# Linear attention with a feed-forward block: loading q and k as they are and casting them on the engines, with a new order of work

## The chip, the core and the metric

The kernel runs on one core of one Trainium2 chip. The metric is the device time of one execution in microseconds; smaller is better. TensorE (PE) does the matmuls, VectorE (DVE), ScalarE (ACT) and GpSimd (POOL) the elementwise work, and SyncE (SP) mostly issues transfers. Each engine works through its own queue in order.

## The reference

Inputs are q, k and v of shape (8, 8, 576, 64), that is batch, head, token and channel, a matrix w_phi (64 x 128), a gain g (512) and the two weights w1 (512 x 2048) and w2 (2048 x 512). All are float32, and the output is (8, 576, 512) in float32.

```python
def phi(x):
    proj = einsum('bhsd,df->bhsf', x, w_phi)
    proj = proj - max(abs(proj), axis=-1, keepdims=True)
    return concatenate([exp(proj), exp(-proj)], axis=-1)
q_p, k_p = phi(q), phi(k)
kv  = einsum('bhsf,bhsd->bhfd', k_p, v)
z   = sum(k_p, axis=2)
num = einsum('bhsf,bhfd->bhsd', q_p, kv)
den = einsum('bhsf,bhf->bhs', q_p, z)[..., None] + 1e-06
x   = (num / den) with the heads side by side        # (8, 576, 512)
xn  = (x - mean(x)) / sqrt(var(x) + 1e-6) * g
out = x + maximum(xn @ w1, 0) @ w2
```

## The kernel before, in words

**Tiling.** The work is cut into 32 units, n = 0 to 31. A unit is one head position of two batches (in the first half of the kernel) or two heads, so that two sequences of 576 tokens fill the 128 partitions as 9 tiles of 128: 8 full tiles ("main") and one tile that is shared by the last 64 tokens of both ("tails", or "mixed"). Eight units make a pair of batches. When a pair's attention is done, its tokens go through layer norm and the feed-forward block (`moe_block`), in blocks of two or three tiles of 128 tokens: `L1307` is the first layer's matmul (hT_ps from xT and w1), `L1337` the second layer's (ch_ps from hT and w2). So attention of one pair and the feed-forward work of the pair before lie side by side.

**Steps of one unit.** (1) Loads of k, q and v: `load_main` for the eight full tiles, `load_tails` for the tails of four units at a time, both through `issue` (L516) on SP. (2) q and k are turned so that the channel lies on the partitions. For n < 8 (`a_trans`, L684 and L692) PE transposes and DVE or ACT copies out of PSUM. For n of 8 and more (`a_trans_dma`) a transposing DMA on SP does it (L766), from a bf16 copy of q and k of 1152 columns: k main, q main, and the mixed tile of both (`cast_mixed`, run by DVE at L747, ACT at L751 or POOL at L753, 128 x 128). (3) k's features (`a_k`): projections pk (L828) and n_bank (L786, L787), their largest magnitude by DVE (`m`, L834 and L790), exponentials on ACT (`eb`, L844 and L799), and the scaled values `vv` on POOL (L856, L865, L869). (4) kv (L1025, L1030). (5) q's features (`a_q` or `a_qt`: L973, L978, L990, L997). (6) num, its copy and division on DVE (numc, L1087 and L1092; rden, L1096) and POOL (x and xs, L1102). Half of the shared tile has to move to other partitions: ACT issues that transfer (x<-xs, L1162). The statistics of layer norm follow on DVE (st, L1220).

**bf16 of q and k, before.** For n of 8 and more, `load_cast` (L598) has GpSimd issue a DMA for each of k and q that reads float32 and writes bf16. It writes into places of 1152 columns inside the three float32 buffers `qk0` to `qk2`, which the first eight units no longer need (`place`, `b16_of`, `freed`), nine in all. Five units ahead of the turned one they may be issued. v has four buffers of its own (`VB`), of two units each.

**Order of work.** Nobody writes the order of instructions down: `add` and `dma` put operations with their engines, an estimate of their duration, dependencies and a rank into the object `Order`, and `Order.run` is a list scheduler that plays the program forward. Whenever an engine is free it takes the waiting operation of lowest rank; where several engines may do an operation (a tuple such as ("DVE", "ACT", "POOL")), the first to come free takes it. The rank is the latest time by which the operation should be done (worked out backward from its users) and an offset from the table `OFF` (by stage and step), or a fixed number for the first loads. DMAs have rings of limited depth in this model, and GpSimd's counts twice as deep in both kernels:

```python
full = op.dma and out.get(op.dma[0], 0.0) + op.dma[1] > self.RING * (1 + (engine == "POOL"))
```

SP's loads for units 4 to 7 are held behind a small read of w1's second part, and those from unit 8 on behind one of w2's first part (`gate`, L528), so that they don't come ahead of the weights. w1 and w2 are loaded by POOL with a cast to bf16, 512 KB at a time (L651 for w2). While PE has nothing else to do early on, it gets matmuls without use[...] (L1537).

Of the kernel before, what the change touches and what calls it, by code (L numbers as in the profile page):

```python
# [17 lines left out]
def bcast(ap: bass.AP, dim: int, n: int) -> bass.AP:  # L18
# [11 lines left out]
        0: 92.8, 1: 85.3, 2: -3301.7, 3: -3074.5, 4: 39.4, 5: 575.5, 6: -409.6, 7: 15.1,  # L30
        8: -3043.8, 9: -3397.9, 10: -8.4, 12: -2030.6, 13: -226.3, 14: 37.5,
    },
    "gln": {
        0: 142.3,
    },
    "k": {
        1: 91, 2: 352.8, 3: 1027.1, 4: -300.7, 5: -347.8, 6: -303.3, 7: -15.4, 8: 86.1, 9: -803.6,
        10: 307.3, 11: 67, 12: 872.6, 14: 68.9,
    },
    "k.copy": {  # L40
        0: 27.5, 1: 624.4, 2: 1020, 3: -41.9, 4: -146.3, 5: -130.6, 6: -93.2, 7: -12.2,
    },
    "k.em": {
        0: 66.7, 1: -12.4, 2: -2704.1, 3: -5.5, 4: 2583.9, 5: 720, 6: 527.6, 7: 686.5, 8: 39.7,
        9: 1215.1, 10: 22.4, 11: -37.6, 12: -46.9, 13: 19.3, 14: -59.6,
    },
    "k.exp": {
        0: 188.2, 1: 599.5, 2: -1722.2, 3: 1885.9, 4: 237, 5: 319.5, 6: 867.4, 7: -1027.3, 8: 71.8,
        9: -954.6, 10: 387.6, 11: 330.1, 12: -2543.4, 13: 63.5, 14: -1109,
    },  # L50
    "k.max": {
        0: 1569, 1: -946.9, 2: 273.7, 3: -20.5, 4: 114.3, 5: 327.6, 6: 1009.3, 7: 1002.8, 8: -0.8,
        9: 1094.3, 10: 10.7, 11: 59, 12: -68.6, 13: -951.5, 14: -1127.6,
    },
    "k.trans": {
        0: -7.2, 1: -1022.5, 2: -632.1, 3: -783.7, 4: -590.8, 5: -463.7, 6: 32.6, 7: -241.5,
    },
    "kv": {
        0: 195.3, 1: 553, 2: -28, 3: -16.8, 4: 270.9, 5: -60.9, 6: 223.5, 7: -39.9, 8: 365.9,
        9: -223.3, 10: -4.4, 11: 20.5, 13: 781.1, 14: -117.9,  # L60
    },
    "kv.copy": {
        0: 237.8, 1: 62, 2: 2860.6, 3: 321.8, 4: 63.3, 5: 2519.7, 6: -15.2, 7: 158.4, 8: -131.4,
        9: -19.3, 10: -60.7, 11: -587.9, 12: -21.5, 13: -167.8, 14: 75.9,
    },
    "ln": {
        1: -186.3, 3: -357.5, 5: 320.2, 7: 225.2, 9: 872.1, 11: 348.5, 12: -181.6, 13: 9.5,
        14: 504.1,
    },
    "load": {  # L70
        0: 156.7,
    },
    "load.k": {
        13: 485.9, 14: 14.4,
    },
    "load.q": {
        12: -258.4, 13: -36.4, 14: -10.1,
    },
    "mixed": {
        0: -130.9, 1: 150.4, 2: 88.2, 3: 843.9, 4: -116.4, 5: -307.5, 6: -40.2, 7: 826.8, 8: -91.9,  # L80
        9: -92.9, 10: -88.2, 11: -759.1, 12: -1174.8, 13: 671.4, 14: 538.1,
    },
    "mixed.exp": {
        0: 927.2, 1: 863, 2: 1200.3, 3: -3220.2, 4: -589.9, 5: -59.5, 6: 740.3, 7: 376.2,
        8: -1565.6, 9: 1094.8, 10: 177.3, 11: -410.5, 12: -3506.5, 13: -1650.3, 14: -105.6,
    },
    "mixed.max": {
        0: -192.1, 1: -703.2, 2: -4.1, 3: -338.5, 4: 2.6, 5: -110.2, 6: -686.6, 7: -22.7, 8: -884,
        9: -2824.2, 10: -192.1, 11: -325.5, 12: -2773, 13: -359.5, 14: -96.5,
    },  # L90
    "num0": {
        0: 668.5, 1: 34.9, 2: -83.4, 3: 342.5, 4: 198.5, 5: -1847.5, 6: -169.5, 7: -294.1,
        8: -20.2, 9: -175.7, 10: 80.8, 11: -1536.1, 12: -48.4, 13: -960, 14: 329,
    },
    "num0.dve": {
        0: 467.7, 1: -325.6, 2: 1058.4, 3: -480.5, 4: -143.5, 5: -456.9, 6: 380.8, 7: 367.2,
        8: -351.2, 9: 1035.8, 10: -367.2, 11: 206.3, 12: -1071.3, 13: -466.6, 14: -343.4,
    },
    "num0.put": {
        0: 158.5, 1: 162.1, 2: 714.5, 3: 1000, 4: 2127.5, 5: 919.3, 6: 170.2, 7: 534.6, 8: 380,  # L100
        9: -292.9, 10: 618.1, 11: -171.9, 12: -129.4, 13: -653.3, 14: -2.8,
    },
    "num1": {
        0: 64.3, 1: -596, 2: -654, 3: -332.2, 4: -1102.9, 5: 475.6, 6: -590.7, 7: -265.9,
        8: -276.4, 9: -9.7, 10: -480.3, 11: -935.2, 12: -521.5, 13: 777.3, 14: 1011.8,
    },
    "num1.dve": {
        0: 84.4, 1: -186.2, 2: -460.6, 3: -1840.9, 4: -2161.8, 5: -395.2, 6: -105.8, 7: -549.4,
        8: -2.1, 10: 97.7, 11: -25.5, 12: -2301.1, 13: -1093.4, 14: -1.7,
    },  # L110
    "num1.put": {
        0: -179.5, 1: -61.8, 2: 860.1, 3: 859.5, 4: 319.2, 5: 1040.7, 6: 995.3, 7: -110.8, 8: 32.3,
        9: -352.4, 10: -61.7, 11: -84, 12: -1.1, 13: -1343.5, 14: 97.8,
    },
    "q.copy": {
        0: 330.4, 1: 30.2, 2: 127.5, 3: -31.8, 4: -79.4, 5: -134.6, 6: -426.1, 7: 529.3,
    },
    "q.em": {
        4: 45.3, 5: -61.4, 6: -188.6, 7: 270.2, 8: 315.4, 9: -17.4, 10: 711.1, 11: 298.7, 12: 22.3,
        13: -76.3, 14: 190.2,  # L120
    },
    "q.max": {
        4: -193.9, 5: -101.7, 6: -240.1, 7: -51.2, 8: -277.1, 9: 20.7, 10: 28.1, 11: -94.7,
        12: -13.8, 13: 92.4, 14: -11.3,
    },
    "q.trans": {
        0: 45.5, 1: -159.9, 2: -531.4, 3: -292.7, 4: -479.2, 5: 176.8, 6: -2243.6, 7: 121,
    },
    "q0": {
        0: 79.7, 1: -34.4, 2: -5.9, 3: -201.1,  # L130
    },
    "q0.em": {
        0: 76.9, 1: 41.6, 2: 606.2, 3: 231.2,
    },
    "q0.max": {
        0: 825, 1: 421.3, 2: 60, 3: 1085.5,
    },
    "q1": {
        0: 197.7, 1: -2405.6, 2: -288.3, 3: -2131.6,
    },  # L140
    "q1.em": {
        0: 238.1, 1: -58.7, 2: -5.1, 3: 4.8,
    },
    "q1.max": {
        0: 427.7, 1: 596.9, 2: 514.4, 3: -33,
    },
    "qt": {
        4: 43, 5: 53.1, 6: -128.5, 7: -1504.6, 8: -3097.5, 9: -1391.5, 10: 114.9, 11: -626.5,
        12: -2970.3, 13: -7.3, 14: -54.6,
    },  # L150
    "rstd": {
        0: 91.5, 8: -236.3, 13: -445.4, 14: 145.7,
    },
    "tails.exp": {
        4: -752.5, 5: -3.9, 6: -0.8, 7: 208.6, 8: 178.4, 9: 354.6, 10: 602.6, 11: -955.4,
        12: -21.2, 13: 639, 14: 303.5,
    },
    "tails0": {
        0: 131.9, 1: -217.5, 2: -9.9, 3: -31.5,
    },  # L160
    "tails0.exp": {
        0: 154.5, 1: -6.8, 2: 62.7, 3: -457.1,
    },
    "tails1": {
        0: 362.3, 1: 805.6, 2: -360.7, 3: 151.6,
    },
    "tails1.exp": {
        0: 149.3, 1: 342, 2: -76.5, 3: 132.1,
    },
    "trans": {  # L170
        8: -2185.6, 10: -214.5, 11: 486.6, 12: 2328, 13: 336.2, 14: 2841.3,
    },
    "vv": {
        0: 1911, 1: -32.9, 2: 1483.8, 3: -49.4, 4: -503, 5: -400, 6: 190.2, 7: 127.9, 8: -262.5,
        9: -99.4, 10: -2335.1, 11: -1439.8, 12: -298.5, 13: -874.4, 14: -529.5,
    },
    "w1": {
        12: -982.9,
    },
    "x.copy": {  # L180
        0: 42.2, 1: -374.1, 2: 474.8, 3: -258.7, 4: -65, 5: 735.5, 6: -171, 7: -70.5,
    },
    "x.trans": {
        0: 934.9, 1: 1052.1, 2: 752.8, 3: 133.9, 4: 1973, 5: 59, 6: 1165, 7: 495.3,
# [11 lines left out]
class Order:  # L196
# [31 lines left out]
    def backward(self):  # L228
        for op in reversed(self.ops):
            us = sum(op.us) / len(op.us) + op.lag  # L230
            if op.dma:
                us += op.dma[1] * op.dma[2] + self.START + self.LAND
            users = [o for o in op.users if not (o.dma and o.engines == ("POOL",))]
            late = min((o.late for o in users), default=1000.0) - us
            op.late = late if op.due is None else min(late, op.due)
# [129 lines left out]
def kernel(  # L365
# [38 lines left out]
    NBUF, VB = 3, 4  # L404
# [44 lines left out]
    for i in range(VB):  # L449
        v_bufs.append(consts.tile([P, HG, MX * D], FP32, name=f"v{i}"))  # L450
# [30 lines left out]
    qkT_bufs = [consts.tile([P, ST], BF16, name=f"qkT{i}") for i in range(QB)]  # L481
    wst = consts.tile([P, F], BF16, name="wst")
# [55 lines left out]
    def load_main(key, n, nu, rank, queue):  # L538
# [4 lines left out]
        slot = g % (VB if key == "v" else NBUF)  # L543
        buf = v_bufs[slot] if key == "v" else qk_bufs[slot][:, "qk".index(key)]
        dst = buf[:, u0 : u0 + nu, :]
        us = range(u0, u0 + nu)
        if pair < SPLIT:
# [7 lines left out]
                [(key + str(half), slot, u) for u in us for half in range(2)]  # L555
# [5 lines left out]
        for half in range(2):  # L561
            b, h, _ = heads(pair, i, half)
            src = bass.AP(
                tensor=t.tensor, offset=t.offset + (b * H + h) * S * D,
                ap=[[4 * D, P], [S * D, nu], [1, 4 * D]],
            )
            issue(
                queue, rank, dst[:, :, half * 4 * D : (half + 1) * 4 * D], src,
                [(key + str(half), slot, u) for u in us], 131072 * nu, gated=gate_of(n),
            )  # L570

    def place(n):
        i = (n - QK_DMA) % (3 * NBUF)
        return i, (i // 3 + 1) % NBUF

    def b16_of(n):
        i, j = place(n)
        flat = qk_bufs[j].rearrange("p a u f -> p (a u f)").bitcast(BF16)
        return flat[:, i % 3 * ST : i % 3 * ST + ST]

    def freed(n):
        if n >= QK_DMA + 3 * NBUF:
            return []
        return [("freed", place(n)[1], u, i) for u in range(HG) for i in range(2)]

    def load_cast(key, n):

        t, i = {"q": q, "k": k}[key], "qk".index(key)
        b, h, _ = heads(n // H, n % H, 0)
        src = bass.AP(  # L590
            tensor=t.tensor, offset=t.offset + (b * H + h) * S * D,
            ap=[[4 * D, P], [S * D if n // H < SPLIT else H * S * D, 2], [1, 4 * D]],
        )
        dst = b16_of(n)[:, i * 512 : (i + 1) * 512].rearrange("p (a f) -> p a f", a=2)
# [980 lines left out]
```

## Time and profile before

| | |
|---|---|
| time, median of 3 runs | 385.69 us (384.36 to 385.82) |
| the profiled execution | 385.82 us, of which the span 384.0 us |
| TensorE clock granted, mean | 0.996 |
| PE busy | 361.3 us, 94% |
| DVE, ACT, POOL busy | 287.3, 233.0, 193.8 us |
| first layer's matmuls L1307, second layer's L1337 | 151.9 and 149.9 us |
| POOL's 48 issues of casting loads (L598) | 24 of 727 ns for k, 24 of 749 ns for q |
| casting loads, from issue to landing, median | k 6.6, q 5.2 us |
| transposing DMAs of q and k (L766) | 24, median 4.6 us to landing |

The page gives busy time by engine, then the span in 40 slices of 9.6 us, a digit being tenths of busy time. A group's row has the line, the engine, the operation, what it writes and reads, the number of instructions, then busy time in us, the mean of one in ns, the idle time of the engine ahead of it and what ended that. A row of the waits has the engine and line that waited, what it waited for, the total in us, the number of times and the longest. Issuing a DMA isn't counted as busy in the first section.

### The profile page before, as it was taken

What the parts mean: (1) busy time and instruction counts of PE and PEld (TensorE: products, weight loads), DVE (VectorE), ACT (ScalarE), POOL (GpSimd) and SP (SyncE); (2) the same over time, 40 slices, a digit from 0 to 9 for tenths busy, and PEclk for the clock granted to TensorE, in tenths of its full rate; (3) what the DMA queues carried; (4) which work ended last, traced back from release to release, by engine and by line L of the source; (5) the groups of instructions that cost most, each with busy time, mean ns of one, the idle gap of its engine ahead of it and who ended that gap; (6) DMA issues with size and microseconds to landing.
All of it is one profiled execution on the core that took longest, in us unless ns stands there. A gap on an engine that the chain in (4) does not pass through costs nothing.

```text
span 384.0 us, 9310 instructions
## 1 busy us (share of the span) xinstructions
PE 361.3 (94%) x3559; PEld 231.0 (60%) x3559; DVE 287.3 (75%) x630; ACT 233.0 (61%) x549; POOL 193.8 (50%) x391
## 2 busy tenths in 40 slices
PE   8899988868989899999999999999999999999995
PEld 8789766524756566655756665665665555555543
DVE  6689977738979798888888896978877956454522
ACT  4879977546879798997867769675665522000000
POOL 2754899735587999895775563432462100000000
PEclk9999999998999999999999999999999999999999
DMA  6998399990699999998977508315100252110102
GB/s 187 270 214 301 58 178 227 175 208 6 142 188 164 199 146 194 185 146 190 152 158 120 137 29 140 76 22 76 46 30 29 43 123 68 29 55 29 54 28 84
DMA packets 93101, 47.08 MB, mean 123 GB/s; under 512 B 59520, under 2 KB 88576, under 8 KB 93056
## 3 DMA queue, kind: packets, MB, share of 16 engines
q1 hardware_dynamic: 74112, 35.60, 41.0%
q0 software_dynamic: 17280, 10.49, 20.5%
q10 hardware_dynamic: 1664, 0.39, 0.5%
q8 instruction: 28, 0.46, 0.5%
q14 instruction: 17, 0.14, 0.1%
HBM read 36.77 MB, written 9.44 MB: 120 GB/s over the span
## 4 chain that ended last, share of the span: by engine, by line
PE 70%; DMA 14%; POOL 5%; SPq 4%; DVE 3%; ACT 2%; issue 1%; DVEq 0%; ACTq 0%; POOLq 0%
PE ch_ps L1337 27%; PE hT_ps L1307 25%; DMA qkT<-qk 4%; PE n_bank L1030 3%; SPq L516 3%; DMA qx<-in_q_dram 3%; PE pk L828 3%; PE num L1073 2%; PE n_bank L1537 2%; POOL vv L856 2%; POOL x L1102 2%; DMA x<-xs 2%; PE pq L973 2%; DMA qk<-in_k_dram 2%; DMA w<-in_moe_w_ch_dram 2%
## 5 line engine op out<-in xcount | busy, mean ns | idle before, releaser
L1307 PE MATMUL hT_ps<-xT,w 128*128 128x384 bf16 (+1 forms) x832 | 151.9, 313 | 4.4 <-ACT hT L1317 2.1
L1337 PE MATMUL ch_ps<-w,hT 128*128 128x512 bf16 (+1 forms) x592 | 149.9, 375 | 0.6 <-DVE hT L1315 0.6
L1307 PEld LDWEIGHTS <-w 128*128 128x128 bf16 x832 | 76.9, 98 | 52.8 <-issue 7.6
L1315 DVE TENSOR_SCALAR hT<-hT_ps 128x384 bf16<-128x384 f32 (+1 forms) x137 | 72.0, 528 | 45.6 <-PE hT_ps L1307 44.1
L1102 POOL TENSOR_TENSOR x<-numc,rden 128x192 bf16<-128x192 f32 (+4 forms) x112 | 49.8, 461 | 73.5 <-DVE rden L1096 62.0
L856 POOL TENSOR_TENSOR vv<-v,em 128x512 bf16<-128x512 f32 x60 | 62.7, 1045 | 42.5 <-issue 18.6
L1337 PEld LDWEIGHTS <-hT 128*128 128x128 bf16 x592 | 54.8, 98 | 45.2 <-issue 3.2
L1317 ACT ACTIVATE hT<-hT_ps 128x384 bf16<-128x384 f32 (+1 forms) x71 | 32.5, 457 | 65.7 <-PE hT_ps L1307 65.2
L844 ACT ACTIVATE eb<-pk 128x1024 bf16<-128x1024 f32 x64 | 65.1, 1033 | 6.0 <-DVE m L834 3.8
L997 ACT ACTIVATE ea<-pt 128x1024 bf16<-128x1024 f32 x56 | 56.7, 1026 | 14.1 <-PE pt L978 13.6
L834 DVE TENSOR_REDUCE m<-pk 128x8 f32<-128x1024 f32 x32 | 38.9, 1217 | 4.5 <-PE pk L828 4.4
L990 DVE TENSOR_REDUCE m<-pq 128x8 f32<-128x1024 f32 x28 | 34.0, 1215 | 4.1 <-PE pq L973 4.1
L1344 DVE SCALAR_TENSOR_TENSOR o<-ch_ps,rstd,x 128x512 f32<-128x512 f32 (+1 forms) x37 | 26.8, 729 | 13.0 <-PE ch_ps L1337 9.7
L1220 DVE BATCH_NORM_STATS2 st<-x 128x6 f32<-128x256 bf16 (+1 forms) x52 | 25.4, 515 | 7.4 <-DMA x<-xs 5.5
L1073 PEld LDWEIGHTS <-ea 128*128 128x128 bf16 x512 | 25.1, 97 | 8.1 <-issue 0.7
L1030 PE MATMUL n_bank<-vv,eb 128*128 128x65 bf16 x512 | 26.8, 194 | 0.0
L1244 ACT ACTIVATE xc<-x,mv 128x512 bf16<-128x512 bf16 x32 | 21.8, 734 | 6.7 <-DVE o L1344 5.1
L1030 PEld LDWEIGHTS <-eb 128*128 128x128 bf16 x512 | 22.3, 98 | 5.5 <-issue 2.2
L869 POOL TENSOR_TENSOR vv<-vx,em 128x130 bf16<-128x130 f32 x63 | 25.2, 400 | 0.0
L1537 PE MATMUL n_bank<-wz 128*128 128x120 bf16 x306 | 23.7, 228 | 0.6 <-ACT KV L1039 0.5
L828 PE MATMUL pk<-wbk,qkT 128*128 128x256 bf16 x128 | 19.8, 279 | 4.2 <-DVE m L990 4.2
L1537 PEld LDWEIGHTS <-wz 128*128 128x128 bf16 x306 | 20.1, 105 | 0.7 <-issue 0.5
(91 smaller groups left out, 451.4 us busy)
## 6 DMA issues: line engine op xcount, KB each, us to landing
out_dram<-o SPq DMA_DIRECT2D x31, 256.0 KB, 2.5
v<-in_v_dram SPq DMA_DIRECT2D x24, 256.0 KB, 3.8
w<-in_moe_w_ch_dram POOLq DMA_DIRECT2D x8, 512.0 KB, 10.3
qk<-in_k_dram POOLq DMA_DIRECT2D x24, 128.0 KB, 6.6
qk<-in_q_dram POOLq DMA_DIRECT2D x24, 128.0 KB, 5.2
qk<-in_k_dram SPq DMA_DIRECT2D x8, 256.0 KB, 5.4
qk<-in_q_dram SPq DMA_DIRECT2D x8, 256.0 KB, 6.5
v<-in_v_dram SPq DMA_DIRECT2D x4, 512.0 KB, 9.3
```

The lines of the kernel that those rows point to most:

```text
L834: nc.vector.reduce_max(out=u["m"][:, 1, 0:MX], in_=u["pk"], axis=AX.X, apply_absolute_value=True)
L844: nc.scalar.activation(u["EB"][:, t, 0:MX, :], u["pk"], AF.Exp, scale=(1.0, -1.0)[t])
L856: eng.tensor_tensor(out=u["vv"][:, t, 0:MX, 0:D], in0=vb[:, hh, :].rearrange("p (c d) -> p c d", d=D), in1=bcast(e[:, 0:MX], 2, D), op=ALU ...
L990: nc.vector.reduce_max(out=out, in_=ps, axis=AX.X, apply_absolute_value=True)
L997: nc.scalar.activation(u["EA"][:, t, :], u["pt", None], AF.Exp, scale=(1.0, -1.0)[t])
L1030: nc.tensor.matmul(ps[:, t, c // 4, :], EB[:, t, c, :], vv[:, t, c, :], start=False, stop=(t == 0 and c == MX - 1), skip_group_check=True,)
L1073: nc.tensor.matmul(ps[t][:, i, :], ea(u, t, c), KV[:, t, c // 4, :], start=True, stop=True,)
L1102: nc.gpsimd.tensor_tensor(out=dst, in0=st["numc"][ps_, at, 0:D], in1=bcast(st["rden"][ps_, at], 2, D), op=ALU.mult,)
L1307: nc.tensor.matmul(st["ps"], w1_sb[:, kc, jj * P : (jj + 1) * P], xT_bufs[xj][:, kc : nt * KC : KC, :], start=(kc == 0), stop=(kc == KC - 1),)
L1315: nc.vector.tensor_relu(h_sb[:, 0 : nt * P], st["ps"])
L1337: nc.tensor.matmul(ch[t, c][:, cols], hT[jj][:, rt * P : (rt + 1) * P], w2_sb[:, jj, cols], start=(jj == 0), stop=(jj == JC - 1),)
L1537: nc.tensor.matmul(warm, wz, wz[:, 0:WN], start=False, stop=False, skip_group_check=True)
```

## The change

1. `load_cast`, `place`, `b16_of` and `freed` are gone. k and q of units 8 to 31 are loaded by SP as float32 with `load_main`, like v, two units at a time into the three groups of buffers (NBUF). These are 40 DMAs more on SP and 48 fewer on POOL.
2. The bf16 copy is made by the engines: two tiles b16_0 and b16_1, used in turn (n % 2), and `cast_main`, which casts k and q separately, 128 x 512 each. DVE does it as a tensor_reduce with max over one element, ACT as a copy, POOL as a multiplication by one. The transposing DMA waits for both and for the mixed cast.
3. v has three groups of buffers instead of four.
4. g's load is issued by SP ahead of the tails of units 4 to 7 and not after them.
5. w2's four loads have ranks of -5 to -2, so that POOL issues them one after the other; before, six casting loads stood between the second and the third, and two more before the last.
6. `backward` takes all users into account; before, it left out users that are DMAs of POOL.
7. All offsets in OFF are new, so the order of instructions is another one on every engine. The scheduler gives the 48 new casts to DVE (14), ACT (11) and POOL (23); the mixed casts go from 11, 4 and 9 to 6, 9 and 9. The matmuls that do useful work are the same[...].

```diff
-            users = [o for o in op.users if not (o.dma and o.engines == ("POOL",))]
-            late = min((o.late for o in users), default=1000.0) - us
+            late = min((o.late for o in op.users), default=1000.0) - us
...
-    NBUF, VB = 3, 4
+    NBUF = 3
...
+    b16_bufs = [consts.tile([P, ST], BF16, name=f"b16_{i}") for i in range(2)]
...
-    def load_cast(key, n):
...
-        dst = b16_of(n)[:, i * 512 : (i + 1) * 512].rearrange("p (a f) -> p a f", a=2)
-        slot = place(n)[0]
-        first = n < QK_DMA + 5
-        dma("POOL", -3.5 + 0.1 * (n - QK_DMA) if first else rk("load." + key, n), 256,
-            lambda: nc.gpsimd.dma_start(out=dst, in_=src),
-            r=[("came", "q", 5) if first else ("turned", n - 5)] + freed(n), w=[("b16", i, slot)],
-            us=0.6, ns=0.05)
...
+        def cast_main(engine, i):
+            cast(
+                engine, b16[:, i * 512 : (i + 1) * 512].rearrange("p (i f) -> p i f", i=1),
+                qk_bufs[u["g"] % NBUF][:, i : i + 1, u["hh"], :],
+            )
...
+        for i in range(2):
+            add(("DVE", "ACT", "POOL"), (0.61, 0.5, 0.98), rank, lambda engine, i=i: cast_main(engine, i),
+                r=loaded(u, "qk"[i])[0:2], w=[("b16", i, n % 2)])
+        dma("SP", rank, 1152, turn, r=[("b16x", n % 2), ("b16", 0, n % 2), ("b16", 1, n % 2)],
...
+    load_weights(order)
     for key in "kqv":
         load_tails(key, 4, next(order), "SP")
-    load_weights(order)
...
-                load_w2(j, (-5.0, -4.0, -3.25, -3.15)[j], [("came", "q", 5)])
+                load_w2(j, -5 + j, [("came", "q", 5)])
...
-            load_main("v", m, HG, rank, "SP")
-        if H <= m < NU:
-            for key in "kq":
-                load_cast(key, m)
+            for key in "kqv":
+                load_main(key, m, HG, rank, "SP")
```

The table `OFF` is replaced as a whole; two of its rows show the manner:

```diff
     "trans": {
-        8: -2185.6, 10: -214.5, 11: 486.6, 12: 2328, 13: 336.2, 14: 2841.3,
+        8: 799.4, 9: -546.4, 10: -650.5, 11: 78.3, 12: -622.9, 13: -375.5, 14: 84.6,
     },
```

## The prediction

> **What bounds the kernel now.** I read the page's slices first, then the windows, the list of waits, the chain between 40 and 130 us and the rows of the operations that the change touches. The slices (sections 1 and 2 of the page):
>
> ```profile
> span 384.0 us, 9310 instructions
> PE 361.3 (94%) x3559; PEld 231.0 (60%) x3559; DVE 287.3 (75%) x630; ACT 233.0 (61%) x549; POOL 193.8 (50%) x391
> PE   8899988868989899999999999999999999999995
> POOL 2754899735587999895775563432462100000000
> PEclk9999999998999999999999999999999999999999
> GB/s 187 270 214 301 58 178 227 175 208 6 142 188 164 199 146 194 185 146 190 152 158 120 137 29 140 76 22 76 46 30 29 43 123 68 29 55 29 54 28 84
> ```
>
> TensorE is the bound, and what it idles lies before slice 13. In windows of 16 us (columns: length, busy time of PE, PEld, DVE, ACT, POOL, then clock, DMA share, GB/s):
>
> ```profile
> 48.00:64.00 16.00, 13.15 (x180) 10.18 (x179) 12.28 (x27) 12.40 (x37) 14.88 (x28) 1.00 1.25 198
> 64.00:80.00 16.00, 14.02 (x152) 8.58 (x148) 12.06 (x31) 6.65 (x12) 13.55 (x35) 1.00 1.03 195
> 80.00:96.00 16.00, 10.75 (x77) 6.27 (x78) 8.87 (x21) 9.96 (x23) 5.39 (x10) 0.89 0.49 84
> 128.00:144.00 16.00, 16.00 (x160) 9.82 (x159) 14.99 (x38) 15.51 (x36) 14.92 (x31) 1.00 1.09 162
> 144.00:160.00 16.00, 16.00 (x177) 10.04 (x175) 14.96 (x35) 13.58 (x30) 14.38 (x32) 1.00 1.10 207
> ```
>
> From 128 us on PE is busy all of the time, so nothing can be won there; but DVE, ACT and POOL are at 14 to 15.5 of 16 us, so something can be lost. Before that, GpSimd is at 14.88 of 16 (48 to 64). The largest single stall is at 84 us:
>
> ```profile
> DVE st L1220 <- DMA x<-xs: 5.5, 1, 5.5
> PE pk L828 <- DVE m L990: 4.2, 1, 4.2
> PE n_bank L1025 <- POOL vv L869: 1.8, 2, 1.5
> ```
>
> DVE waits in order for x<-xs, issued at 79.61 and landed 6.41 us later; the maximum that PE needs stands behind it, and PE stands 4.15 us. After it the granted clock drops: four matmuls L828 take 1.01 us in place of 0.6, in all some 1.6 us more.
>
> [...] the casting loads L598 are on POOL, the transposes L766 on SP. [...] a qx load of SP at 51.87 took 9.27 us beside w2 and the casting loads of POOL. [...] a cast by reduction costs its element count; here 418 ns for 256 elements and 1217 for 1024, 1.04 ns an element.
>
> **The change part by part.** Rows used:
>
> ```profile
> L856 POOL TENSOR_TENSOR vv<-v,em 128x512 bf16<-128x512 f32 x60 | 62.7, 1045 | 42.5 <-issue 18.6 <-ACT em L841 16.5 <-ACT em L850 6.6
> L598 POOL DMA_DIRECT2D qk<-in_q_dram x24 | 18.0, 749 | 0.0
> L598 POOL DMA_DIRECT2D qk<-in_k_dram x24 | 17.4, 727 | 0.0
> L915 DVE TENSOR_REDUCE m<-pq 128x4 f32<-128x512 f32 x8 | 5.4, 679 | 0.8 <-PE pq L910 0.8
> L948 ACT ACTIVATE ea<-pt 128x512 bf16<-128x512 f32 x16 | 9.0, 601 | 1.6 <-PE pt L942 1.6
> qkT<-qk SPq DMA_TRANSPOSE x24, 4.6
> v<-in_v_dram SPq DMA_DIRECT2D x4, 512.0 KB, 9.3
> ```
>
> *GpSimd, −1.5 us (−5 to 0).* 48 issues leave it: 24 × 0.727 + 24 × 0.749 = 35.4 us. The new order of instructions gives it 23 of the 48 casts; by the nearest row, the same operation on as many elements, 23 × 1.045 = 24.0 us. Between 43 and 60 us it issued ten of the loads (7.4 us) and four of w2 (3.1), and stood on the chain with vv behind them; in the new order two casts stand among the vv of heads 4 to 7, and the w2 loads remain. The 1.5 us that PE waited for vv L869 can go; if all behind it comes 5 us earlier, more. A gain of more than 5 is excluded: PE's idle time between 48 and 80 is 16 − 13.15 + 16 − 14.02 = 4.8.
>
> *VectorE and ScalarE, +3.5 us (0 to +9).* They get 14 and 11 casts. By L915 and L948, 14 × 0.68 + 11 × 0.60 = 16.1 us; the small casts of tails move from DVE to ACT (11 to 6, and 4 to 9) at 0.27 and 0.29, which evens out. Spread over about 210 us this is 1.2 us in 16, where the two have 0.5 to 2.4 free. What decides is how late the transposition comes. By the order of instructions I added up PE's work, at this trace's durations, between the last PE instruction that a transposition depends on and the first that needs its result. For the first heads of the second pair it is 18, 28, 22, 9 us before and 8.2 (n=9), 10.7 (n=11), 15.2 (n=8), 8.6 (n=10) after; n=13 has 6.8. The path needs two casts one after the other (about 1.5), the ends of the instructions ahead in both queues (about 1 each) and the transposition: 4.6 median, 8.3 at most, say 5.5; together 9. Then n=9, n=10 and n=13 are late by 0.8, 0.4 and 2.2: 3.4. The upper end has each transposition at 8.3. With two bf16 tiles (n mod 2) in place of nine, a cast also waits for the transposition two heads back; and on SP everything behind a waiting transposition, the next k, q and v loads, waits too.
>
> *SP, nothing to +2, taken in the next item.* 40 more loads at 0.6 us are 24 us over 200 us on a queue that has hardly any work between; their cover is the lead of the loads.
>
> *First loads, +2.5 us (0 to +5).* Before, the bf16 of heads 8 to 10 was asked for at 44.5 to 48. After, k and q of heads 8 and 9 follow the gate on w2 (passed at 49.00), 512 KB each, beside four w2 loads that are now issued together. At the 9.3 us of v's 512 KB they land at 59 and 60. The first cast (k, n=8) stands in POOL's queue between the vv of heads 6 and 7, where POOL came at about 55 to 57; behind it are vv, then x, which the chain needs. DVE's first cast (k, n=9) stands before numc, rden, and the hT that PE waits for. If both come at 57, they wait 2 to 3 us. With 4.3 us (the shortest v load) it is nothing, with 12 it is 5.
>
> *x<-xs, −2 us (−5.7 to 0).* The stall of 4.15 + 1.6 us hung on one order: statistics ahead of the maximum, PE with little work. In the new order an xT copy and hT stand behind the statistics, and PE has about 10 us of second-layer matmuls in reach. I take a stall of 2 to 3 us left[...], and 1 us of it spent again on a later wait.
>
> *g's load, nothing.* Landed at 28.4 and first used at 36.1, without a wait; moved past six tail loads on SP it delays each by one issue, 0.6 us, and these tails are first used at 31.1. *Three v buffers for four:* v is loaded no later than k and q; covered by these. *w2's issue order:* the last comes at about 46 and not 57.55, first used by the second layer; counted above as DMA traffic.
>
> Sum: −1.5 + 3.5 + 2.5 − 2.0 = +2.5, against the profiled execution's 385.8: 388.3. That execution is 0.1 above the median of the runs (385.69), so it needs no correction.
>
> **Rivals.** *Casts hidden, faster, 381.* GpSimd's 10.5 us of issues in 43 to 60 shrink to 3.1 + 2 × 1.05 = 5.2, vv comes 5 us sooner, PE wins back 1.5 to 3 of its 4.8, and the stall at 84 with its slow clock goes (up to 5.7, say 3): −4.5 to −5. For it: POOL is on the chain from 40 to 72, and the stall has nothing to do with capacity. Against: the short leads. It decides if the path of a transposition takes under 8 us, so that none is late. Chance 0.27. *Stalls trade places, no change, 385.7.* The order only shifts which wait shows; from 128 us PE has all it needs. Chance 0.16. *The chain through SP, slower, 395.* Each cast waits for the transposition two heads back, SP's loads queue behind it, and DVE stops in order at a cast whose load has not come: every head of the second and third pair then costs 0.6 us more on PE, 16 × 0.6 = 9.6. For it: 15 of 16 us busy at 128 to 160. Against: later leads are 11 to 50 us. Chance 0.15. My forecast has 0.42.
>
> **How the numbers follow.** A measurement of this kernel tells 0.5% from no change, so the bounds are 383.8 and 387.6. The forecast alone runs from 386 to 392; the range 379.5 to 397 takes in the fast rival with its −5 and the slow one with a little over. Faster is the first rival and little else, 0.27. Same is the second and the forecast's lowest part, 0.18. Slower is the rest, 0.55.
>
> **What would show it.** Right: POOL or DVE waiting at a cast for a load of k or q near 57; PE waits at n=9, 10, 13 that lead to the transposition; the 4.2 us stall at L828 smaller; PE below 16.00 in one of the windows after 128. POOL's busy time should fall by about 11 us, DVE's rise by 8 to 9, ACT's by 8. Wrong: casts at other than 0.68, 0.60 and 1.05 us; first loads landing before 56; PE's idle time from 48 to 96 down by 4 or more without new waits; PE full from 112 on.

## The result, and the profile after

The changed kernel takes 374.44 us (374.14 to 375.42) against 385.75 us for the kernel before on the same chip; the ratio is 0.971, with a 95% interval of 0.9668 to 0.9752. So it is 11.3 us faster, where slower was forecast. Its profiled execution took 375.42 us, with a span of 373.3.

The slices of the page, in the same rows as were shown of before:

```profile
span 373.3 us, 9376 instructions
PE 360.5 (97%) x3555; PEld 230.1 (62%) x3555; DVE 288.7 (77%) x634; ACT 238.5 (64%) x570; POOL 183.1 (49%) x366
PE   8899998998999989999999999999999999999996
POOL 2856668564777678676766655544444100000000
PEclk9999999999999999999999999999999999999999
```

PE does the same work in nearly the same busy time (361.3 before, 360.5 now). What went is idle time of PE, from 384.0 − 361.3 = 22.7 us to 373.3 − 360.5 = 12.8: 9.9 of the 10.7 us by which the span is shorter. The dip at slice 9 is gone, and the clock has no dip there any more (80 to 96 us: 0.89 before, 1.00 now). Windows of 16 us (length, busy time of PE, PEld, DVE, ACT, POOL, clock, DMA share, GB/s), two of the kernel before and then those of the kernel after:

```profile
96.00:112.00 16.00, 14.29 (x172) 10.65 (x170) 13.45 (x30) 14.38 (x38) 10.37 (x23) 1.00 0.74 152
112.00:128.00 16.00, 14.42 (x159) 8.96 (x159) 13.37 (x32) 12.31 (x25) 13.09 (x29) 1.00 1.18 188
```

```profile
48.00:64.00 16.00, 14.78 (x191) 11.78 (x188) 13.53 (x29) 14.45 (x39) 11.63 (x24) 1.00 1.15 252
64.00:80.00 16.00, 15.53 (x156) 8.38 (x156) 13.55 (x33) 8.61 (x17) 8.68 (x26) 1.00 0.74 198
80.00:96.00 16.00, 14.22 (x157) 10.40 (x155) 14.93 (x38) 14.43 (x39) 10.99 (x22) 1.00 0.82 211
96.00:112.00 16.00, 15.93 (x163) 9.73 (x161) 15.24 (x33) 12.03 (x26) 11.71 (x27) 1.00 1.06 251
112.00:128.00 16.00, 16.00 (x165) 9.80 (x162) 15.16 (x34) 16.00 (x37) 11.84 (x22) 1.00 0.97 220
128.00:144.00 16.00, 14.91 (x138) 8.12 (x137) 13.50 (x29) 14.22 (x34) 12.41 (x26) 1.00 1.02 229
```

Over the first 128 us PE is busy for 119.94 us, where it was 109.74. The gain is 3.1 us from 48 to 80, 3.5 from 80 to 96 and 3.2 from 96 to 128; from 128 to 144 a little is given back (1.1). From 80 to 128 us DVE is now busy for 14.9 to 15.2 of 16 us, as it was from 128 to 160 before: work has moved forward. The longest entries of PE's waits are short, and no entry of its matmuls leads to a transposing DMA of q and k:

```profile
PE qkT_ps L645 <- DMA qk<-in_k_dram: 2.0, 3, 1.3
PE n_bank L1500 <- DVE wz L419: 1.0, 1, 1.0
PE pt L946 <- DVE numc L1060: 1.0, 2, 0.6
PE n_bank L993 <- POOL vv L837: 0.8, 2, 0.5
```

One transposition came just in time: issued at 99.75, it landed at 104.36, and the matmuls that read it (pk) began at 104.41; their weight load (PEld) had waited for it for 0.6 us.

The casts have the prices that the prediction used, and POOL and DVE did wait at their first one:

```profile
L712 POOL TENSOR_TENSOR b<-qk,one 128x512 bf16<-128x512 f32 x23 | 23.9, 1041 | 16.6 <-DMA qkT<-b 9.4 <-issue 5.8 <-DMA qk<-in_k_dram 1.4
L706 DVE TENSOR_REDUCE b<-qk 128x512 bf16<-128x512 f32 x14 | 9.5, 679 | 2.3 <-DMA qk<-in_k_dram 1.4 <-DMA qkT<-b 0.8
L710 ACT CAST b<-qk 128x512 bf16<-128x512 f32 x11 | 7.0, 636 | 4.8 <-DMA qkT<-b 3.5 <-POOL x L1070 1.4
```

After the last bar comes the idle time ahead of the group. POOL waited 9.4 us in all for a transposition two heads back to free its bf16 tile, and POOL and DVE 1.4 us each for the first k. Among the waits of PE's matmuls no entry names a cast.

### The profile page after: what moved, and what is told of

Same layout as the page of the kernel before. It is cut to its first block, busy times and chain, and to the rows that moved or that the text cites. A ratio compares the mean times of both kernels' runs of the same rounds, so it can differ in the third digit from the quotient of the medians.

```text
span 373.3 us, 9376 instructions
## 1 busy us (share of the span) xinstructions
PE 360.5 (97%) x3555; PEld 230.1 (62%) x3555; DVE 288.7 (77%) x634; ACT 238.5 (64%) x570; POOL 183.1 (49%) x366
## 4 chain that ended last, share of the span: by engine, by line
PE 67%; ACT 14%; DMA 7%; POOL 5%; issue 3%; SPq 2%; DVE 2%; ACTq 0%; DVEq 0%; POOLq 0%
PE hT_ps L1275 27%; PE ch_ps L1305 23%; ACT eb L812 3%; PE n_bank L998 3%; DMA qkT<-b 2%; ACT ea L965 2%; PE num L1041 2%; DMA xT<-xc 2%; PE pk L796 2%; PE pq L941 2%; POOL x L1070 2%; SPq L509 2%; DMA qk<-in_k_dram 2%; PE n_bank L1503 2%; POOL vv L824 1%
## 5 line engine op out<-in xcount | busy, mean ns | idle before, releaser
L1275 PE MATMUL hT_ps<-xT,w 128*128 128x384 bf16 (+1 forms) x832 | 149.1, 314 | 1.3 <-DVE hT L1283 0.5
L1305 PE MATMUL ch_ps<-w,hT 128*128 128x512 bf16 (+1 forms) x592 | 146.4, 373 | 0.0
L824 POOL TENSOR_TENSOR vv<-v,em 128x512 bf16<-128x512 f32 x62 | 65.0, 1050 | 29.7 <-ACT em L809 17.1
L965 ACT ACTIVATE ea<-pt 128x1024 bf16<-128x1024 f32 x56 | 58.1, 1051 | 11.2 <-PE pt L946 11.1
L712 POOL TENSOR_TENSOR b<-qk,one 128x512 bf16<-128x512 f32 x23 | 23.9, 1041 | 16.6 <-DMA qkT<-b 9.4
L1041 PEld LDWEIGHTS <-ea 128*128 128x128 bf16 x512 | 24.4, 98 | 5.0 <-issue 0.9
L1188 DVE BATCH_NORM_STATS2 st<-x 128x6 f32<-128x256 bf16 (+1 forms) x52 | 24.4, 512 | 0.5 <-POOL x L1070 0.5
L1503 PE MATMUL n_bank<-wz 128*128 128x120 bf16 x302 | 23.8, 225 | 0.7 <-ACT KV L1007 0.7
L1055 DVE TENSOR_TENSOR numc<-num,em 128x390 f32<-128x390 f32 (+2 forms) x36 | 19.2, 533 | 3.1 <-PE num L1041 2.3
```

What stands on the lines that cost most here:

```text
L824: eng.tensor_tensor(out=u["vv"][:, t, 0:MX, 0:D], in0=vb[:, hh, :].rearrange("p (c d) -> p c d", d=D), in1=bcast(e[:, 0:MX], 2, D), op=ALU ...
L965: nc.scalar.activation(u["EA"][:, t, :], u["pt", None], AF.Exp, scale=(1.0, -1.0)[t])
L1041: nc.tensor.matmul(ps[t][:, i, :], ea(u, t, c), KV[:, t, c // 4, :], start=True, stop=True,)
L1275: nc.tensor.matmul(st["ps"], w1_sb[:, kc, jj * P : (jj + 1) * P], xT_bufs[xj][:, kc : nt * KC : KC, :], start=(kc == 0), stop=(kc == KC - 1),)
L1305: nc.tensor.matmul(ch[t, c][:, cols], hT[jj][:, rt * P : (rt + 1) * P], w2_sb[:, jj, cols], start=(jj == 0), stop=(jj == JC - 1),)
```

## The experiments

Two theories. **O**: the gain is the order of work, that is the new table of offsets (OFF); where the cast is done matters little. **L**: the gain is that GpSimd and the DMA engines are rid of 48 casting loads. Every kernel was timed beside the kernel before; differences below are against the kernel before of the same call (385.0 to 386.7 us), and the kernel after stands at −11.3.

### The table without the casting, the casting without the table

The kernel before with the new table, and the kernel after with the old one:

```diff
 # e1: the kernel before
-OFF = OLD_TABLE
+OFF = NEW_TABLE   # and load.k, load.q of the old one
 # e2: the kernel after
-OFF = NEW_TABLE
+OFF = OLD_TABLE
```

> The kernel before (GpSimd's casting loads, four v buffers) with the table of offsets of the kernel after; the offsets of its own load stages are kept. Theory O (the order of work gives the gain): 374 to 380 us. Theory L (taking the casting loads off GpSimd and the DMA engines gives the gain, the offsets only follow it): 383 us or more, since GpSimd still issues 35.4 us of loads and the waits at 48 to 96 us stay.

> The kernel after (float32 loads by SP, casts on the engines) with the table of offsets of the kernel before. Theory O: 385 us or more, as the old order, or worse, since its offsets were not made for the casts. Theory L: 375 to 381 us, most of the gain of 11.3 us without the new offsets.

Measured: 402.7 us (+16.0) and 415.3 us (+28.6). The first is in theory L's open band and the second in theory O's, so the pair contradicts itself: each of these tables fits one way of casting only, and with the other the kernel is far slower than either. The list scheduler's own account says so too: run with these tables, it ends at 387.3 us for e1 and at 404.7 for e2, where it ends at 366.3 and 365.5 for the kernels before and after. The two parts can't be told apart by exchanging them. With no table at all:

```diff
-OFF = NEW_TABLE   # e3: the kernel after
-OFF = OLD_TABLE   # e4: the kernel before
+OFF = {}
```

> The kernel after with an empty table of offsets: every operation ranked by its latest time alone. Read against the same of the kernel before, it compares the two ways of casting with no table on either side. Theory O: the two are within 3 us of each other, both some per cent above their own tables (390 to 410). Theory L: this one is 5 to 12 us faster than the other.

> The kernel before with an empty table of offsets. Theory O: within 3 us of the kernel after without offsets. Theory L: 5 to 12 us slower than that.

Measured: 397.73 us for casting on the engines (ratio to before 1.0285, interval 1.0252 to 1.0318) and 398.13 us for casting loads (1.0321, 1.0267 to 1.0374). The intervals overlap: without a table the two ways can't be told apart, as theory O has it, and against theory L's 5 to 12 us. (Everything else of the change, v's buffers, g's and w2's loads, is in e3 and not in e4.) By the ratios, the old table is worth about 12 us to its kernel and the new one about 22 to its own.

### What the stall at x<-xs was worth

In the kernel before, in its own order, the statistics are taken of another tile, so that DVE doesn't wait for the transfer:

```diff
-            nc.vector.bn_stats(out=pr["st"][:, t, half or 0, :], in_=x[:, t, h0 * D : h1 * D])
+            nc.vector.bn_stats(out=pr["st"][:, t, half or 0, :], in_=x[:, 0 if (pair, t) == (0, MX) else t, h0 * D : h1 * D])
```

> The kernel before in its own order; only the statistics of the first pair's shared tile are taken from the pair's first tile, which is complete by then, so that VectorE does not wait there for x<-xs (this leaves the right statistics of that tile out). If the stall of 4.15 us and the slow clock after it (1.6 us) are worth their full size: 380 us, 5 to 6 below the kernel before. If a later wait takes their place: 384 to 386 us.

Measured: 379.19 us (−5.8; ratio 0.9852, 0.9788 to 0.9917, that is 3.2 to 8.2 us over four executions). The size fits the 4.15 and 1.6 us of the prediction, but the profile shows another course. PE's wait for m is gone. An earlier one has grown from 1.4 to 2.5 us, and in the profiled execution, which at 382.13 us was the slowest of the four, the granted clock falls all the same, from about 81.9 to 85.3 us:

```profile
PE xT_ps L1183 <- ACT xc L1244: 2.5, 1, 2.5
82.00:83.00 1.00, 1.00 (x11) 0.48 (x12) 0.43 (x1) 0.07 (x1) 0.00 (x0) 0.50 1.26 269
84.00:85.00 1.00, 1.00 (x4) 0.41 (x3) 1.00 (x6) 1.00 (x3) 0.00 (x0) 0.50 1.38 198
```

The other three executions have a mean clock of 1.000, where the kernel before has 0.986 to 0.996 in the same call, and took 377.5 to 380.0 us. So the wait was worth 3 to 8 us; that the slow clock hung on the stall of 4.15 us alone is not shown. The same by order alone, with the same work, moves this one instruction behind the next four of DVE when the order is written out:

```diff
+        i = done.index(self.later)          # statistics of pair 0's shared tile
+        op, passed = done.pop(i), 0
+        while passed < 4:
+            passed += done[i].engine == "DVE"
+            i += 1
+        done.insert(i, op)
         for op in done:
```

> The kernel before in its own order, with one instruction moved: VectorE's statistics of the first pair's shared tile stand behind the next four of its instructions, two of them the maxima that TensorE waits for. Nothing is left out. If the stall is a matter of order: 379 to 382 us. If the wait for x<-xs, only moved back, stops the feed-forward work behind it just as long: 384 to 386 us.

Measured: 382.33 us (−3.0; ratio 0.9919, 0.9894 to 0.9944, that is 2.2 to 4.1 us), 0.3 above the first band. A wait is left:

```profile
DVE st L1226 <- DMA x<-xs: 1.9, 1, 1.9
```

PE no longer waits for m (the entry of 4.2 us is gone), but DVE still stands 1.9 us at the statistics, ahead of xT and xc. The clock is at 0.50 here too, from about 80.9 to 84.3 us, behind a wait of PE of 2.1 us. Whether the 1.9 us are why e17 won less than e5 is not shown: the two intervals overlap, and the two profiled executions have spans of 379.8 and 380.4 us. One place in an order of 2,300 operations decides about 3 us. In the kernel after, x<-xs is issued at 78.0 and lands in 2.6 us, and DVE comes to the statistics at 80.96: no wait.

### What GpSimd's time and the casts cost in the new order

```diff
 # e6: ahead of the vv of heads 4 to 24, at t == 0 of scale_main; e9: of heads 6 to 24 only
+                for m in {4: (8, 9, 10), 5: (11, 12)}.get(n, (n + 7,) if 6 <= n <= 24 else ()):
+                    for _ in range(2):
+                        nc.gpsimd.tensor_tensor(
+                            out=spare, in0=gln_sb[:, 0:1].to_broadcast([P, 350]),
+                            in1=one.to_broadcast([P, 350]), op=ALU.mult)
 # e8: in the same places, a casting load of k and one of q to memory
+                    for i, t in enumerate((k, q)):
...
+                        nc.gpsimd.dma_start(
+                            out=spare[2 * (m - 8) + i, :, :].rearrange("p (a f) -> p a f", a=2), in_=src)
 # e7: cast_main
+            for _ in range(2):
                 cast(
...
```

> The kernel after in its own order, with 48 additional multiplications of 128x350 on GpSimd, some 0.7 us each, ahead of the vv of heads 4 to 24: as much time of GpSimd as the removed issues of casting loads took (35 us), six of them ahead of head 4's vv, four ahead of head 5's. Theory L (GpSimd's issue time was what cost): 380 us or more. Theory O (the order): 374 to 377 us.

> The kernel after in its own order with only the later 38 of the 48 multiplications on GpSimd, ahead of the vv of heads 6 to 24 (26 us in all); those ahead of heads 4 and 5 are left out. With all 48 it was 390 us. If GpSimd's time costs only where it stands on the chain of the first pair (43 to 60 us): 375 to 379 us. If it costs everywhere: 385 us or more.

> The kernel after in its own order, each of the 48 casts done twice: 9.5 us more on VectorE, 6.8 on ScalarE, 24 on GpSimd. If the transpositions' leads are as tight as the prediction took them (9 us needed, 6.8 to 8.6 there), each of n=9, 10 and 13 comes about 1.5 us later still: 378 to 382 us. If the casts lie under cover: 374 to 376 us.

> The kernel after in its own order, and 48 casting loads of q and k more, issued by GpSimd ahead of the vv of heads 4 to 24 and written to memory that nobody reads: the issue time and the traffic of the removed loads are both back. Theory L: 382 us or more. Theory O: 375 to 379 us; the difference to the padded kernel is the traffic.

Measured: e6 390.14 us (+5.2, that is 16.5 above the kernel after), e9 384.19 (−0.95; 10.4 above, in neither band), e7 385.83 (+0.85; 12 above, more than either of its bands), e8 406.28 (+21.3; 33 above). The longest wait of PE in e6, and the padding itself:

```profile
PE n_bank L1001 <- POOL vv L845: 13.0, 9, 5.1
L825 POOL TENSOR_TENSOR spare<-gln,one 128x350 bf16<-128x350 f32 x48 | 36.9, 769 | 2.1
```

By the padding alone theory L would seem shown: 36.9 us more of GpSimd cost 16.5, most of it as PE's wait for vv (13.0 us, where the kernel after has 0.8), 6 from the first ten multiplications and 10 from the later 38 (29.2 us). But the other side costs about as much: the casts a second time (POOL 47.7 − 23.9 = 23.8 us more, DVE 9.6, ACT 6.6) cost 12. So in this order GpSimd's issues and the casts, one taken away and the other put in, would nearly cancel, in line with the empty tables. Each of the additions tried here was dear in an order that was made without it. That does not say that the same addition is dear in an order that was made with it, as e11 below shows. In e8 loads stand in place of e6's multiplications; they cost another 16 us in this order. They are not quite the removed ones: they come on top of the float32 loads, and write to main memory and not to on-chip buffers.

### g's load

In the kernel after, only g's load goes back behind the six tail loads:

```diff
     def load_weights(order):
         def gln():
-            nc.sync.dma_start(out=gln_sb, in_=moe_g_ln.rearrange("(kc p) -> p kc", p=P))
+            pass
...
+    def tail_then_gln(dst, src):             # the last tail load, v of units 4 to 7
+        def emit():
+            nc.sync.dma_start(out=dst, in_=src)
+            nc.sync.dma_start(out=gln_sb, in_=moe_g_ln.rearrange("(kc p) -> p kc", p=P))
```

> The kernel after in its own order; only g's load goes back behind the tails of units 4 to 7. Both theories: no difference, 374 to 376 us, since g lands long before its first use.

Measured: 378.63 us (−6.5), 4.8 slower than the kernel after. Both theories missed it. Two waits of this run that the kernel after does not have:

```profile
DVE ngln L604 <- DMA gln<-in_moe_g_ln_dram: 4.5, 1, 4.5
PE pq L887 <- DVE qkT L669: 3.8, 1, 3.8
```

The new order has the negation of g at 24.4 us in DVE's queue, where the old one had it at 36.1. With the load at its old place g lands at 16.1 + 11.2 = 27.3; DVE stands for 4.5 us, and PE for 3.8 behind it. Ahead of the tails it lands at 11.4 + 6.6 = 18.0. The edit that seemed to do nothing is needed by this order of instructions.

### New tables for both

If the order is what counts, the kernel before must be able to be as fast as the kernel after with a table of its own. Tables were searched by annealing from an empty one: offsets were changed a few at a time, the change kept if the list scheduler's own end fell, or, less and less, if it rose a little; e14's search was to reach as low an end as the other tables have.

```diff
 # two rows of e11's table (the kernel before); e13 is another for it, e12 and e14 are for the kernel after
-OFF = OLD_TABLE
+OFF = {
...
+    "k.max": {0: -25.2, 1: 40.1, 2: -47.8, 3: 812.5, 4: 519.9, 5: -361.4, 6: -817.2, 7: -79.4, 8: -386.5, 9: 223.1, 10: -1607.7, 11: 2614.4, 12: -1832.4, 13: -1671.7, 14: -5.8},
...
+    "trans": {8: -5950.3, 9: -14.3, 10: -2467.1, 11: 16.2, 12: -978.9, 13: 2321.7, 14: 596.3},
...
+}
```

> The kernel before with a table of offsets found anew by annealing from an empty table, against the order model's own end (366.7 us there; the table of before has 366.3, that of after 365.5). It shares no offset with the table of before. If the casting loads hold the kernel at 385 us, it is at 383 to 392 us. If the old table's order was an unlucky one of many that the model holds equal: 374 to 382 us.

> The kernel after with a table found anew in the same manner (369.1 us in the order model, 3.6 more than its own table). If casting on the engines gives the gain: 375 to 380 us, below the kernel before with its new table. If it is the order: within 4 us of that, either way.

> The kernel before with another table found from an empty one (other seed; 367.8 us in the order model). If 385 us was an unlucky order: again 373 to 381 us. If the new table of the run before was the lucky one and 385 is what casting loads usually give: 382 us or more.

> The kernel after with another table found from an empty one, this time with as low an end in the order model as the others (366.6 us). If the way of casting doesn't matter: 372 to 381 us, as the kernel before with its new tables. If casting on the engines is worse: above all of those.

| kernel and table | end by the list scheduler, not a time of the chip | measured | gap |
|---|---|---|---|
| before, its own | 366.3 | 385.7 | 19.4 |
| before, e11 | 366.7 | 373.3 | 6.6 |
| before, e13 | 367.8 | 377.8 | 10.0 |
| before, none (e4) | 391.1 | 398.1 | 7.0 |
| after, its own | 365.5 | 374.4 | 8.9 |
| after, e12 | 369.1 | 378.7 | 9.6 |
| after, e14 | 366.6 | 378.8 | 12.2 |
| after, none (e3) | 385.3 | 397.7 | 12.4 |

This speaks for theory O, in the first place by e11. With casting loads, four v buffers, and g's and w2's loads in their old places, e11 has a ratio of 0.9721 to before (0.9688 to 0.9755), the same as the kernel after. It keeps GpSimd's 48 issues, and PE has no dip at slice 9 (rows of its page, of its DMA issues, and a window):

```profile
PE 357.9 (96%) x3531; PEld 230.5 (62%) x3572; DVE 288.3 (78%) x640; ACT 227.3 (61%) x537; POOL 195.2 (53%) x393
PE   8899799999999999999999999999999999999996
qk<-in_k_dram POOLq DMA_DIRECT2D x24, 128.0 KB, 4.9
qk<-in_q_dram POOLq DMA_DIRECT2D x24, 128.0 KB, 5.5
48.00:80.00 32.00, 30.92 (x359) 21.41 (x360) 27.56 (x66) 21.84 (x48) 26.97 (x58) 1.00 1.28 192
```

From 48 to 80 us, where the prediction looked for GpSimd's share, PE is busy for 30.92 us here with the issues, and for 30.31 in the kernel after without them. So what was won there does not need the issues to go.

Orders that the scheduler holds within 3.6 us of each other lie from 373.3 to 385.7 on the chip. The old table is the outlier, by its gap of 19.4, and e5 names 3 to 8 us of that; the rest of it is open. e12 lies 5.4 above e11: theory O allowed 4, and the other theory asked for a time below e11's. And both searched tables of the kernel after lie above both of the kernel before (by 0.9 to 5.5 us): if the way of casting has a share of its own, these few tables put it against the change. Their means differ by 3.2 us, two tables of one kernel by up to 4.5.

### Measured prices in the scheduler

```diff
 # used for the search only; e15 from the own table of after, e16 from that of e11
+ each DMA lands 1.2 us later; ACT's exponentials 0.1 us longer; casts as measured
+ GpSimd's issue of a casting load 0.74 us, not 0.6
```

> The kernel after with a table found against the order model with measured prices (exponentials 0.1 us longer, casts as measured) and 1.2 us later landings of every DMA, starting from its own table. If the model's optimism on these is what separates model and chip: 368 to 373 us, faster than both kernels. If not: 373 to 380 us.

> The kernel before with a table found in the same manner, GpSimd's issue of a casting load also at the measured 0.74 us instead of 0.6. If the model's optimism is what separates model and chip: 369 to 374 us. If not: 374 to 382 us.

Measured: 386.72 us (+1.4) and 407.95 us (+22.6). Both missed their bands. But the two runs don't test the prices: these served the search only, and the kernels still make their order by the old ones. By these the scheduler ends at 375.9 us (e15) and 401.5 (e16), so the tables do not fit it, and the gaps to the chip, 10.9 and 6.4 us, are like the others of the table. What separates the scheduler from the chip is open. The best version, e11, can't be told from the kernel after by its interval; none that is faster than both was found.

## Why the prediction was wrong, point by point

Three steps failed. The two costs, +3.5 for late transpositions and +2.5 for the first loads, did not reach PE. The stall at x<-xs, taken at −2, was worth 3 to 8 us by e5. And the new order as such stood at nothing beyond the waits named, while a new table alone makes the kernel before 10.8 us faster (e11: 373.3, by its ratio of 0.9721).

- **Prices: right.** Casts were taken at 1.045, 0.68 and 0.60 us and measured 1.041, 0.679 and 0.636. POOL's busy time fell by 10.7 (11 forecast). ACT's rose by 5.5 where 8 was said and DVE's by 1.4 where 8 to 9 was said, in part since fewer of the other copies fell to DVE (KV 18 to 15, xT 9 to 6, vv 4 to 2).
- **First loads, +2.5: the wait was right, its cost wrong.** k of head 8 was reckoned to land at 59. POOL and DVE stood at it until 59.9, 1.4 us each, in the places named. PE's idle time from 48 to 64 fell from 2.85 to 1.22 us all the same, and none of its waits there leads to a cast. I had carried an engine's wait over to the end without asking what PE had in hand, and I had put that question for x<-xs only.
- **Transpositions, +3.5: wrong.** The leads of 6.8 to 8.6 us were set against a need of 9. No matmul of PE waits for a transposition in the kernel after (one weight load does, 0.6 us, with no time to spare); the kernel before had a wait of 1.5 us. A term that was too large is the landing: 5.5 was taken from a median of 4.6 and a maximum of 8.3; in the kernel after it is 3.9 in the median and 6.1 at most. How much of the rest is the queue ahead of the casts, taken at 2, was not measured by itself. The wait for the tile two heads back exists (9.4 us on POOL), and no wait of PE leads to it.
- **x<-xs, −2: mis-sized.** By e5 the wait was worth 5.8 us (3.2 to 8.2). It went altogether; I kept 2 to 3 us of it, by estimate without a slow clock, and took 1 us as spent again. The 6.4 us of its landing were taken as given; they became 2.6. That the stall of 4.15 us caused the slow clock was taken from one trace; in e5 and e17 the clock fell without that stall, behind waits of 2.5 and 2.1 us.
- **GpSimd, −1.5: within its bounds, its cause not shown.** PE won back 3.1 us of its 4.8 from 48 to 80. But e11 wins back as much there with all 48 issues in place, so that it was their going is not shown.
- **96 to 128 us: left out.** PE's idle time there fell by 3.2 us. In before most of it were two waits, for o and for a transposition, that no step of the prediction held:

```profile
PE hT_ps L1307 <- DVE o L1344: 1.5, 1, 1.5
PE n_bank L786 <- DMA qkT<-qk: 1.5, 1, 1.5
```

- **g, nothing: wrong for the new order.** The cover named (first use at 36.1) was the old order's. e10 has it at 4.8 us.
- **Rivals.** "Casts hidden, faster" has the outcome, at 381 in place of 374: its condition was that no transposition is late, and none held up a matmul. It took the stall at 3 us and left out the 96 to 128 us. (Its two terms add up to −4.5 to −6, not −5.) Its reason for the first term, GpSimd's issues, is not shown, as said above. "The chain through SP" did not occur.
- **The error behind these.** Part 7 of the change, all offsets new, was priced only through waits that I could point at in the old trace. The runs show that it is a term of its own: three orders of the kernel before that its scheduler ends within 1.5 us of each other differ by up to 12 us on the chip. A term of that size belonged into the range; 379.5 as the lower end was too high by 5.

## What to carry to other kernels

When a change comes with a new order from a scheduler, time the two ways with the same treatment of the order (no table on either side, or a fresh search on both) before crediting the mechanism: here the way of casting by itself was worth nothing that these runs could measure, and an order about 11 us. Ask of the largest stall first whether it is a matter of queue order: here an instruction that waited for a transfer stood in front of one that the bounding engine needed, and moving it four places won 3 us. And before calling a moved load free, look up where its first reader stands in the new order, not in the old.

## What the runs showed of the hardware

**Landings beside casting loads.** Within one order of instructions the 24 transposing DMAs of q and k landed later with GpSimd's casting loads beside them. Their medians from issue to landing are 3.9 us in the kernel after and 3.6 to 3.7 in e6, e7, e9 and e10, none above 6.1; with 48 casting loads added (e8) it is 5.2, and 8.5 at most. It depends on the order too: with casting loads in all of them, it is 4.6 in the kernel before, 3.3 in e11 and 3.1 in e13. For the four small transfers x<-xs (32 KB) no such effect is shown: their medians are 2.4 to 4.0 us without casting loads in the same order (4.0 in e9), and 3.9 with them. Nor do these loads bound a kernel by themselves: e11 has them and runs in 373.3.

**The slow clock.** In the kernel before the granted clock of PE fell to 0.50 at 88.0 us, 3.9 us into the pause of 4.15 us, and was back at 1.00 at 91.4. It fell to 0.50 also behind pauses of 2.5 us (e5, from about 81.9 to 85.3) and 2.1 us (e17, from about 80.9 to 84.3). It stayed at 1.00 after a pause of 1.4 us (the kernel before, 79.7 to 81.1). How long a pause, or how little work, brings the clock down, these few cases don't show.
